# Second branch: queries projected before keys; x turned in pairs; nine early Z sums; fifth chunks prepared ahead

## The chip, the core and the metric

The kernel runs on one core of a Trainium2 chip. The core has a matrix engine (TensorE: PE for matmuls and transposes, PEld for its weight loads), VectorE (DVE), ScalarE (ACT), GpSimd (POOL) and SyncE (SP, which here only issues DMAs). Each engine takes its instructions in program order, and engines wait for each other through semaphores. The metric is device time in microseconds (us) of one execution; smaller is better.

## The reference

Two attention branches over the same tokens (S = 2048, D = 640, 32 heads of 20) are mixed by a gate. Cut to what matters here:

```python
x = A_x
g = sigmoid((x * gate_w).sum(-1, keepdims=True))
return g * A(x) + (1 - g) * B(x)

# A: linear attention with learned features
q, k, v = split_heads(x @ wqkv)
pq, pk = q @ w_phi, k @ w_phi                       # per head, 20 x 20
phi_q = concat(softmax(pq), softmax(-pq))
phi_k = concat(softmax(pk), softmax(-pk))
kv, z = phi_k.T @ v, phi_k.sum(tokens)
A = ((phi_q @ kv) / (phi_q @ z + 1e-6)) @ wo

# B: four segments of 512 tokens, a causal softmax and a memory (M, z)
phi = lambda t: where(t > 0, t + 1, exp(t))
for s in range(4):
    a_dot = causal_softmax(qs @ ks.T * 20 ** -0.5) @ vs
    a_mem = (phi(qs) @ M) / (phi(qs) @ z + 1e-6)
    outs.append(sigmoid(beta) * a_mem + (1 - sigmoid(beta)) * a_dot)
    M, z = M + phi(ks).T @ vs, z + phi(ks).sum(tokens)
B = concat(outs) @ wo_B
```

The inputs and the output are bf16.

## The kernel before

Tokens go in 16 chunks of 128, the 640 features in five blocks of 128 (KC), the 32 heads in eight groups of four. Both stages around the change run under an order written out by hand: instructions stand on each engine's queue as the code emits them. Lines are those of the kernel before.

**Start.** Weights of the first branch's keys come by DMA in five row blocks. For each block n, step T (`emit_foldT`, L175) transposes it on PE and evicts it; step M (`emit_foldM`, L182) multiplies it by `Wphi`, a block-diagonal copy of `w_phi` that POOL writes in five products (`emit_Wphi`, L142), and ACT evicts the product into `WkA`. Step X (`emit_xT`, L192) transposes one chunk of x (five PE transposes) and DVE copies it into `xTf`. The loop at L299 gives their order. All of these, the warm-up transposes (L296) and later `pk`, `pv`, `kv_ps`, `pq` use one PSUM pool of four double-bank buffers (tag `w2`), taken in turn.

**First branch, keys and values.** `emit_a1` (L226) runs 16 times: key and value projections of a chunk on PE (ten matmuls each, L232), two exponentials on ACT, sums and reciprocals on DVE, normalisation on POOL into `EkSn`, from where a DMA spreads it over the 32 tiles of `Z`. Then `kv` is formed on PE (L373) in tiles that DVE masks into `kvn` (L380), a tile's PSUM buffer coming free with that product. On DVE the 31 sums of the Z tiles (`emit_zadd`, L256, one instruction each) stand in three runs around the `kvn`: tiles 1 to 11, 12 and 13, 14 to 31. PE turns the sum later (`emit_z`), and DVE makes the denominators' operand `kvd` from it.

**First branch, queries.** `emit_pq` (L386) projects queries, ACT takes both exponentials (L398). A loop over the 16 chunks (from L570) forms numerators (`num`, L440), scales them on DVE (`tt`, L486), adds them on POOL (`oA`, L592) and turns the result by DMA into `oTA`. Between them `emit_next_half` puts projections of the second branch for its first chunks (L539, a half being 320 of 640 columns), evicted by ACT: the list `halves` holds chunks 0 to 3 of k and q and 0 to 7 of v, and ends with k and q of chunk 4. A finished k or q chunk is turned by DMA (`emit_turn`, L551) into `kTs` or `qTs`.

**Second branch.** 32 steps (4 segments, 8 groups of heads) go in 16 pairs; the loop is at L896. A pair has five bursts: each puts scores for four heads into two PSUM tiles (L666) and ACT takes two exponentials of 128x1024 into `PT` (L670); POOL zeroes the triangle above the diagonal (L677). Between the bursts the pair's other work is dealt out in the order of a string of `PLAN` (L882), by its estimated time:

- h: a projection half for the next segment (L854), evicted by DVE (L860); after a chunk's second half of q or k, its turn by DMA is issued, and its feature step is queued up. The order of the halves of segments 2 and 3 is `CHUNKED` (L870), that of segment 1 `FIRST_SEG`.
- x, y: DVE finishes phi of the oldest waiting k (x) or q (y) chunk: a minimum with 1 (L829), then maximum and sum (L830). The exponential they need is issued on ACT by `run_first(waiting[..])` (L920): one waiting q chunk behind burst 0, one waiting k chunk behind burst 2; in pair 0 behind bursts 2 and 3.
- z: SP issues the turn of phi(q) of that chunk into `xTf` (L839), out of the single staging tile `phiq_st`.
- A, B, C, D: the matmuls with V (L722, `pv_items`), for C and D also those with the memory (`mem_items`, L730 and L735) and the end of a step (`emit_epi`, L741): `rec`, `td`, `mtmp` on DVE, `oB`, `Msb`, `Mbd` on POOL. A and D belong to the pair's first step, B and C to the second step of the pair before. Their PSUM tile `nda` is single, so the next step's first matmul waits for `mtmp`, its last reader.
- o, f: output projections (L800); t, u: turns of finished outputs by DMA.

Of the kernel before, what the change touches and what calls it, by code (L numbers as in the profile page):

```python
# [7 lines left out]
ACT = mybir.ActivationFunctionType  # L8
# [7 lines left out]
def kernel(  # L16
# [15 lines left out]
    nc = tc.nc  # L32
# [109 lines left out]
    def emit_Wphi(j):  # L142
        h0, h1 = TH[j]
        nc.gpsimd.tensor_tensor(out=Wphi[:, j, 0:h1 - h0, :],
                                in0=Wc[:, j:j + 1, :].to_broadcast([P, h1 - h0, DH]),
                                in1=wmask[:, j, h0:h1, None].to_broadcast([P, h1 - h0, DH]),
                                op=ALU.mult)

    for j in range(KC):
        emit_Wphi(j)  # L150
# [41 lines left out]
    def emit_xT(sc, eng):  # L192
        tp = aps.tile([P, KC, P], BF16, name="xtp", tag="w2")
        for c in range(KC):
            nc.tensor.transpose(out=tp[:, c, :], in_=x_nat[sc // 2][:, sc % 2, c * P:(c + 1) * P],
                                identity=ident_b)
        eng(out=xq[:, sc // 4, :, sc % 4 * P:(sc % 4 + 1) * P], in_=tp)  # L197
# [28 lines left out]
    def emit_a1(sc):  # L226
        pk, pv = w2tile("pk"), w2tile("pv")
        for ps, W, n in ((pk, WkA, 320), (pv, WvA, 321)):
            for bk in range(2):
                for c in range(KC):  # L230
                    rhs = WvA[:, c, bk, :] if W is WvA else WkA[:, c, bk * 320:(bk + 1) * 320]
                    nc.tensor.matmul(ps[:, bk, 0:n], lhsT=key_tokens(c, sc), rhs=rhs,  # L232
                                     start=(c == 0), stop=(c == KC - 1))
# [62 lines left out]
    warm = aps.tile([P, KC, P], BF16, name="warm", tag="w2")  # L296
    for n in range(25):
        nc.tensor.transpose(out=warm[:, n % KC, :], in_=ident_b, identity=ident_b)
    for step in ("T0", "T1", "T2", "M0", "M1", "T3", "T4", "M2", "X0", "M3", "X1", "M4", "X2", "X3"):  # L299
        n = int(step[1])  # L300
        if step[0] == "T":
            emit_foldT(wnat_k, WkT, n, nc.scalar.copy if n == 1 else nc.vector.tensor_copy)
        elif step[0] == "M":
            emit_foldM(WkT, WkA, n)
        else:
            emit_xT(n, nc.vector.tensor_copy)
# [94 lines left out]
    emit_zadd(range(1, 12))  # L401
# [9 lines left out]
    emit_zadd(range(12, 14))  # L411
# [131 lines left out]
    def emit_half(pool, part, sc, half, eng, **kw):  # L543
        ps = pool.tile([P, 320], F32, name="proj", **kw)
        emit_half_mm(ps, part, sc, half)
        psv = ps.rearrange("p (h d) -> p h d", d=DH)
        hs = slice(half * 16, (half + 1) * 16)
        dst = vBs[(sc // 4) % 2][:, sc % 4] if part == "v" else stages[part][sc % 2]
        eng(out=dst[:, hs, 0:DH], in_=psv)

# [7 lines left out]
    for vB in vBs:  # L558
        nc.gpsimd.memset(vB[:, :, :, DH:DH + 1], 1.0)
    halves = [(part, c, half) for n in range(4) for part, c in (("k", n), ("q", n), ("v", n), ("v", 4 + n))  # L560
              for half in range(2)] + [(part, 4, half) for part in "kq" for half in range(2)]

    def emit_next_half():
        if halves:
            emit_half(last_pps if len(halves) % 3 == 1 else pps, *halves.pop(0), nc.scalar.copy)

    nums = [emit_num(0, 0)]
    emit_next_half()
    nums.append(emit_num(0, 1))
    for ch in range(NCH):  # L570
# [3 lines left out]
        part, c = (("k", ch // 4), ("q", ch // 4), ("v", ch // 4), ("v", 4 + ch // 4))[k]  # L574
# [26 lines left out]
        if k < 2:  # L601
            emit_turn(part, c, kT0 if part == "k" else qT0)
# [15 lines left out]
    with ExitStack() as bctx:  # L618
# [3 lines left out]
        Eqf = Eq0.rearrange("p j s t -> p (j s t)")  # L622
        kTs, qTs = ([t, Eqf[:, n * G * L:(n + 1) * G * L].rearrange("p (g t) -> p g t", g=G)]
                    for n, t in enumerate((kT0, qT0)))
# [12 lines left out]
        phiq_st = Eqf[:, 2 * G * L:2 * G * L + 2 * L].rearrange("p (h e) -> p h e", e=32)  # L637
# [182 lines left out]
        def features(part, sc):  # L820
# [3 lines left out]
            def exps():  # L824
                ek = bw.tile([P, H, DH], BF16, name="ek")
                nc.scalar.activation(out=ek, in_=src, func=ACT.Exp)  # L826
# [40 lines left out]
        def half_items(s, order):  # L867
            return [half_item(part, 4 * s + c, half) for part, c in order for half in range(2)]

        CHUNKED = [(part, c) for c in range(4) for part in "kqv"]  # L870
# [11 lines left out]
        PLAN = {0: ("hhhhoyzoAoxD", "hhBhyhzCooxAoD", "hhBhyhzCooxAoD", "ooBoyozCooxAoD"),  # L882
                1: ("hhBhhChxAhDtt", "hhBhyhzCfhhxAD", "hhBhyhzCfhhxADt", "hhBhyhzCfhhxAD"),
                2: ("hhBhyhzChxAhDt",) + ("hhBhyhzCfhhxADt",) * 3,
                3: ("fByfzCffADtt", "fBftCfftAD", "fBftCfffAD", "ufBfCfffAD")}
# [6 lines left out]
        for part in "kq":  # L892
            emit_turn(part, 4, (kTs if part == "k" else qTs)[1])
            features(part, 4)
        prev = None
        for dstep in range(NSEG * G // 2):  # L896
# [21 lines left out]
            for n, burst in enumerate(bursts(a, b)):  # L918
                burst()
                if n in ((0, 2) if dstep else (2, 3)):  # L920
                    run_first(waiting["kq"[n == (0 if dstep else 2)]])
                while items and (n == 4 or done + items[0][0] / 2 < (n + 1) * share):
                    w, fn = items.pop(0)
                    fn()
                    done += w
# [141 lines left out]
```

## Time and profile before

| what | us |
|---|---|
| median of 3 runs (lowest, highest) | 327.36 (327.29, 328.22) |
| the profiled execution, its own time | 326.66 |
| its span in the trace | 324.9 |
| exponentials of the scores (ACT, L670), 160 of them | 154.0 |
| matmuls with V (PE, L722) | 41.7 |
| exponentials of the waiting chunks (ACT, L826) | 0.74 each, 20 in the second branch's pairs |
| start to first key projection (PE, L232) | 10.7 |
| first exponential of the second branch's scores | 133.5 |
| start of pair 8 / of pair 9 | 223.2 / 235.5 |

The profile is of one execution: its span runs from the first to the last instruction in the trace, and its own time is 1.8 us longer. The costliest groups after the exponentials, with columns line, engine, operation, output<-input, count, then busy us and mean ns of one, then idle time ahead of it and what ended most of that:

```profile
L666 PE MATMUL st_ps<-Z 32*128 32x512 bf16 (+3 forms) x256 | 24.7, 299 | 3.7 <-ACT PT L670 3.1
L486 DVE TENSOR_TENSOR tt<-num,rr 128x640 f32<-128x640 f32 x32 | 24.8, 802 | 4.9 <-POOL rr L479 2.2
L800 PE MATMUL proj<-WkA,oTA 128*128 128x320 bf16 x160 | 27.1, 300 | 0.0
```

The last column tells who kept an engine waiting: the scores on PE wait for ACT to free their PSUM tiles, the scaled numerators wait for a POOL product, and the output projections wait for nothing.

### The profile page before, as it was taken

What the parts mean: (1) busy time and instruction counts of PE and PEld (TensorE: products, weight loads), DVE (VectorE), ACT (ScalarE), POOL (GpSimd) and SP (SyncE); (2) the same over time, 40 slices, a digit from 0 to 9 for tenths busy, and PEclk for the clock granted to TensorE, in tenths of its full rate; (3) what the DMA queues carried; (4) which work ended last, traced back from release to release, by engine and by line L of the source; (5) the groups of instructions that cost most, each with busy time, mean ns of one, the idle gap of its engine ahead of it and who ended that gap; (6) DMA issues with size and microseconds to landing.
All of it is one profiled execution on the core that took longest, in us unless ns stands there. A gap on an engine that the chain in (4) does not pass through costs nothing.

```text
span 324.9 us, 9495 instructions
## 1 busy us (share of the span) xinstructions
PE 308.9 (95%) x3904; PEld 212.9 (66%) x3904; DVE 223.0 (69%) x447; ACT 252.1 (78%) x322; POOL 211.2 (65%) x310
## 2 busy tenths in 40 slices
PE   7999999999999999989999999999799999999995
PEld 6788877964577788555565566655566656555663
DVE  2577997997799797377768567776575665454463
ACT  4677888138845555899999999999799889898853
POOL 8688599202268789647657667677776787666550
PEclk9999999999999999999999999999999999999999
DMA  7948935691015867766231455633555553422122
GB/s 226 201 112 195 209 98 154 194 366 39 0 34 105 117 106 124 147 121 84 52 67 32 87 55 67 139 56 65 87 79 92 103 104 39 113 67 58 46 87 81
DMA packets 91812, 34.19 MB, mean 105 GB/s; under 512 B 79866, under 2 KB 91770, under 8 KB 91770
## 3 DMA queue, kind: packets, MB, share of 16 engines
q1 hardware_dynamic: 91194, 32.95, 49.5%
q10 hardware_dynamic: 576, 0.66, 0.7%
q8 instruction: 30, 0.49, 0.6%
q14 instruction: 12, 0.10, 0.1%
HBM read 6.42 MB, written 2.62 MB: 28 GB/s over the span
## 4 chain that ended last, share of the span: by engine, by line
PE 41%; ACT 20%; issue 2%; DVE 1%; DMA 1%; SPq 0%; ACTq 0%; DVEq 0%
ACT PT L670 19%; PE st_ps L666 9%; PE proj L800 8%; PE proj L854 7%; PE nda L722 6%; PE proj L539 4%; PE num L440 2%; DMA xTf<-Eq 1%; PE nda L730 1%; PE nda L735 1%; ACT ek L826 1%; PE nda L976 1%; PE st_ps L976 0%; PE den L450 0%; DVE rec L747 0%
## 5 line engine op out<-in xcount | busy, mean ns | idle before, releaser
L670 ACT ACTIVATE PT<-st_ps 128x1024 bf16<-128x1024 f32 x160 | 154.0, 1025 | 15.1 <-PE st_ps L666 12.4
L677 POOL TENSOR_SCALAR_AFFINE_SELECT PT<-PT 128x512 bf16<-128x512 bf16 (+1 forms) x130 | 86.8, 685 | 48.7 <-ACT PT L670 48.4
L722 PEld LDWEIGHTS <-PT 128*128 128x128 bf16 x1280 | 40.1, 96 | 11.1 <-issue 6.4
L722 PE MATMUL nda<-vB,PT 128*128 128x21 bf16 x1240 | 41.7, 173 | 1.4 <-DVE mtmp L765 0.9
L244 POOL TENSOR_TENSOR EkSn<-Ek,krec 128x1280 bf16<-128x1280 bf16 x16 | 37.5, 2361 | 8.3 <-DVE krec L243 8.1
L854 PEld LDWEIGHTS <-xTf 128*128 128x128 bf16 x300 | 26.3, 97 | 16.0 <-issue 7.2
L860 DVE CAST Z<-proj 128x320 bf16<-128x320 f32 x44 | 20.7, 486 | 19.7 <-PE proj L854 19.4
L232 PEld LDWEIGHTS <-xTf 128*128 128x128 bf16 x240 | 27.1, 113 | 6.2 <-DVE xTf L197 0.7
L240 DVE TENSOR_REDUCE ksum<-Ek 128x64 f32<-128x1280 bf16 x16 | 23.6, 1475 | 8.0 <-ACT Ek L236 8.0
L236 ACT ACTIVATE Ek<-pk 128x640 bf16<-128x640 f32 x32 | 20.8, 702 | 10.6 <-PE pk L232 9.8
L666 PE MATMUL st_ps<-Z 32*128 32x512 bf16 (+3 forms) x256 | 24.7, 299 | 3.7 <-ACT PT L670 3.1
L486 DVE TENSOR_TENSOR tt<-num,rr 128x640 f32<-128x640 f32 x32 | 24.8, 802 | 4.9 <-POOL rr L479 2.2
L592 POOL TENSOR_TENSOR oA<-tt 128x640 bf16<-128x640 f32 x16 | 24.6, 1545 | 4.7 <-DVE tt L486 3.4
L800 PE MATMUL proj<-WkA,oTA 128*128 128x320 bf16 x160 | 27.1, 300 | 0.0
L666 PE MATMUL st_ps<-Eq 32*128 32x512 bf16 (+3 forms) x256 | 24.6, 299 | 2.2 <-ACT PT L670 1.7
L398 ACT ACTIVATE Eq<-pq 128x1024 bf16<-128x1024 f32 x20 | 19.4, 1021 | 5.4 <-PE pq L393 5.4
L762 POOL TENSOR_TENSOR oB<-td 128x320 bf16<-128x320 f32 x22 | 18.9, 861 | 5.9 <-DVE td L759 4.9
L800 PE MATMUL proj<-WvA,oT 128*128 128x320 bf16 x120 | 22.3, 300 | 0.5 <-DVE oTA L809 0.5
L393 PE MATMUL pq<-xTf,WqA 128*128 128x512 bf16 x100 | 22.1, 379 | 0.0
L759 DVE TENSOR_TENSOR td<-nda,rec 128x640 f32<-128x640 f32 x23 | 19.0, 825 | 2.1
L539 PEld LDWEIGHTS <-xTf 128*128 128x128 bf16 x180 | 16.3, 97 | 4.4
L232 PE MATMUL pk<-WkA,xTf 128*128 128x320 bf16 x120 | 18.3, 299 | 0.6 <-DVE xTf L197 0.6
(166 smaller groups left out, 551.7 us busy)
## 6 DMA issues: line engine op xcount, KB each, us to landing
Z<-EkSn SPq DMA_DIRECT2D x32, 160.0 KB, 2.7
out_dram<-orow SPq DMA_DIRECT2D x8, 160.0 KB, 2.0
out_dram<-oTA SPq DMA_DIRECT2D x6, 160.0 KB, 1.9
WvA<-in_A_wqkv_dram SPq DMA_DIRECT2D x2, 400.0 KB, 6.8
WkB<-in_B_wk_dram SPq DMA_DIRECT2D x1, 800.0 KB
WqB<-in_B_wq_dram SPq DMA_DIRECT2D x1, 800.0 KB, 7.0
WvB<-in_B_wv_dram SPq DMA_DIRECT2D x1, 800.0 KB, 8.6
WkA<-in_A_wo_dram SPq DMA_DIRECT2D x1, 800.0 KB, 11.3
```

What stands on the lines that cost most here:

```text
L232: nc.tensor.matmul(ps[:, bk, 0:n], lhsT=key_tokens(c, sc), rhs=rhs, start=(c == 0), stop=(c == KC - 1))
L240: nc.vector.tensor_reduce(out=ksum, in_=Ek.rearrange("p s (h f) -> p (s h) f", f=DH), axis=AX.X, op=ALU.add)
L244: nc.gpsimd.tensor_tensor(out=EkSn[:, sc].rearrange("p s (h f) -> p (s h) f", f=DH), in0=Ek.rearrange("p s (h f) -> p (s h) f", f=DH), in1 ...
L486: nc.vector.tensor_tensor(out=tt[:, sgn].rearrange("p (b h) d -> p b h d", b=2), in0=ps, in1=csb, op=ALU.mult)
L539: nc.tensor.matmul(ps, lhsT=xq[:, sc // 4, cc, sc % 4 * P:(sc % 4 + 1) * P], rhs=W[:, cc, half * 320:(half + 1) * 320], start=(cc == 0), s ...
L592: nc.gpsimd.tensor_tensor(out=oA.rearrange("p (h d) -> p h d", d=DH), in0=tt[:, 0], in1=tt[:, 1], op=ALU.add)
L666: nc.tensor.matmul(ps[:, i - i0, o:o + L - c * P], lhsT=kT[32 * i:32 * i + 32, c * P:(c + 1) * P], rhs=qT[32 * i:32 * i + 32, c * P:L], st ...
L670: nc.scalar.activation(out=PT[:, i0:i0 + 2], in_=ps, func=ACT.Exp, scale=SCALE_B)
L677: nc.gpsimd.affine_select(out=v, in_=v, pattern=[[0, n_i], [1, P]], compare_op=ALU.is_ge, fill=0.0, base=0, channel_multiplier=-1)
L722: nc.tensor.matmul(nd[:, j, i], lhsT=block(st, c)[:, i, (j - c) * P:(j - c + 1) * P], rhs=vB[:, c, 4 * st.g + i, :], start=(c == 0), stop= ...
L800: nc.tensor.matmul(ps, lhsT=oT[:, k % KC], rhs=W[:, k % KC, hs], start=(k == 0), stop=(k == n - 1))
L854: nc.tensor.matmul(ps, lhsT=xq[:, sc // 4, k, sc % 4 * P:(sc % 4 + 1) * P], rhs=W[:, k, half * 320:(half + 1) * 320], start=(k == 0), stop ...
```

## The change

Six things change; no instruction is dropped from the computation, and PE's matmuls and transposes keep their number.

1. `emit_Wphi` takes an engine. Blocks 0 and 2 go to DVE, 4, 1 and 3 to POOL, in the order 0, 4, 2, 1, 3.
2. `emit_xT` takes a pair of chunks: ten transposes into one double-bank PSUM tile, one copy by DVE instead of two. X0 and X1 now stand ahead of M3 and M4 in the steps, T4 is evicted by ACT, and the first `emit_a1` goes through its matmuls by input block with the two column halves inside.
3. The warm-up uses two PSUM tiles instead of one and x two instead of four, so every later user of the four `w2` buffers is shifted by one.
4. The first run of Z sums covers tiles 1 to 9 instead of 1 to 11, and the second tiles 10 to 13.
5. k and q of chunk 4 move in `halves` ahead of v of chunks 3 and 7; their turns are issued in the loop of the first branch; their exponentials are taken on ACT in the loop's last two rounds, into the places where phi is formed, and x and y of pair 0 find them done. Pair 0's two places for an exponential (now behind bursts 0 and 2) serve the next chunks. The last half is evicted by DVE.
6. `CHUNKED` becomes q, k, v for each chunk. In `PLAN` y and z move to the end of the pairs of segments 1 and 2 and x, where there is one, to their middle; in pair 0 an o moves behind y and z, and in pair 12 y and z go. From segment 1 on, burst 0 issues the exponential of k and burst 2 that of q; segment 0 keeps q first.

Counted on ACT, the exponentials of waiting chunks fall by pair as follows (pairs 0 to 12): before 2, 2, 2, 2, 1, 2, 2, 2, 1, 1, 1, 1, 1; after 1, 2, 2, 1, 1, 2, 2, 2, 2, 1, 1, 1, 0.

```diff
--- before.py
+++ after.py
@@ -139,15 +139,15 @@
     kvd = Aw.tile([P, 2, KC, H, 2], BF16, name="kvd")
     for j, (h0, h1) in enumerate(TH):
         nc.gpsimd.tensor_copy(out=wmw[:, j, 0:h1 - h0], in_=wmask[:, j, h0:h1])
-    def emit_Wphi(j):
+    def emit_Wphi(j, eng):
         h0, h1 = TH[j]
-        nc.gpsimd.tensor_tensor(out=Wphi[:, j, 0:h1 - h0, :],
+        eng.tensor_tensor(out=Wphi[:, j, 0:h1 - h0, :],
                                 in0=Wc[:, j:j + 1, :].to_broadcast([P, h1 - h0, DH]),
                                 in1=wmask[:, j, h0:h1, None].to_broadcast([P, h1 - h0, DH]),
                                 op=ALU.mult)
 
-    for j in range(KC):
-        emit_Wphi(j)
+    for j, eng in ((0, nc.vector), (4, nc.gpsimd), (2, nc.vector), (1, nc.gpsimd), (3, nc.gpsimd)):
+        emit_Wphi(j, eng)
...
@@ -189,12 +189,15 @@
                              start=(n in FIRST), stop=(n in LAST))
         nc.scalar.copy(out=dst[:, ic, :].rearrange("p (b n) -> p b n", b=2), in_=ps[:, :, 0:320])
 
-    def emit_xT(sc, eng):
-        tp = aps.tile([P, KC, P], BF16, name="xtp", tag="w2")
-        for c in range(KC):
-            nc.tensor.transpose(out=tp[:, c, :], in_=x_nat[sc // 2][:, sc % 2, c * P:(c + 1) * P],
-                                identity=ident_b)
-        eng(out=xq[:, sc // 4, :, sc % 4 * P:(sc % 4 + 1) * P], in_=tp)
+    def emit_xT(n):
+        pair = w2tile("xtp")
+        for u in range(2):
+            tp = pair[:, u].bitcast(BF16)[:, 0:D].rearrange("p (c t) -> p c t", c=KC)
+            for c in range(KC):
+                nc.tensor.transpose(out=tp[:, c, :], in_=x_nat[n][:, u, c * P:(c + 1) * P], identity=ident_b)
+        dst = xq[:, 0, :, 2 * n * P:2 * (n + 1) * P].rearrange("p c (u t) -> p u c t", u=2)
+        src = pair.bitcast(BF16)[:, :, 0:D].rearrange("p u (c t) -> p u c t", c=KC)
+        nc.vector.tensor_copy(out=dst, in_=src)
...
@@ -226,11 +229,11 @@
     def emit_a1(sc):
         pk, pv = w2tile("pk"), w2tile("pv")
         for ps, W, n in ((pk, WkA, 320), (pv, WvA, 321)):
-            for bk in range(2):
-                for c in range(KC):
-                    rhs = WvA[:, c, bk, :] if W is WvA else WkA[:, c, bk * 320:(bk + 1) * 320]
-                    nc.tensor.matmul(ps[:, bk, 0:n], lhsT=key_tokens(c, sc), rhs=rhs,
-                                     start=(c == 0), stop=(c == KC - 1))
+            by_row = [(c, bk) for c in range(KC) for bk in range(2)]
+            for c, bk in by_row if sc == 0 else sorted(by_row, key=lambda t: t[1]):
+                rhs = WvA[:, c, bk, :] if W is WvA else WkA[:, c, bk * 320:(bk + 1) * 320]
+                nc.tensor.matmul(ps[:, bk, 0:n], lhsT=key_tokens(c, sc), rhs=rhs,
+                                 start=(c == 0), stop=(c == KC - 1))
...
@@ -293,17 +296,17 @@
             op=ALU.mult)
         return omgh_b, CM
 
-    warm = aps.tile([P, KC, P], BF16, name="warm", tag="w2")
+    warm = [aps.tile([P, KC, P], BF16, name="warm", tag="w2") for _ in range(2)]
     for n in range(25):
-        nc.tensor.transpose(out=warm[:, n % KC, :], in_=ident_b, identity=ident_b)
-    for step in ("T0", "T1", "T2", "M0", "M1", "T3", "T4", "M2", "X0", "M3", "X1", "M4", "X2", "X3"):
+        nc.tensor.transpose(out=warm[n % 2][:, n % KC, :], in_=ident_b, identity=ident_b)
+    for step in ("T0", "T1", "T2", "M0", "M1", "T3", "T4", "M2", "X0", "X1", "M3", "M4"):
         n = int(step[1])
         if step[0] == "T":
-            emit_foldT(wnat_k, WkT, n, nc.scalar.copy if n == 1 else nc.vector.tensor_copy)
+            emit_foldT(wnat_k, WkT, n, nc.scalar.copy if n in (1, 4) else nc.vector.tensor_copy)
         elif step[0] == "M":
             emit_foldM(WkT, WkA, n)
         else:
-            emit_xT(n, nc.vector.tensor_copy)
+            emit_xT(n)
...
@@ -398,7 +401,7 @@
             nc.scalar.activation(out=Eq[:, sgn, :], in_=pqf, func=ACT.Exp, scale=1.0 - 2.0 * sgn)
         Eqs[qb, j] = Eq
 
-    emit_zadd(range(1, 12))
+    emit_zadd(range(1, 10))
     PAIRS = [(js, sgn) for js in ((0, 3), (1, 4)) for sgn in range(2)]
     for js, sgn in PAIRS:
         for j in js:
@@ -408,7 +411,7 @@
             emit_kv(j, sgn, range(14, NCH))
...
-    emit_zadd(range(12, 14))
+    emit_zadd(range(10, 14))
...
@@ -541,12 +544,15 @@
                              start=(cc == 0), stop=(cc == KC - 1))
 
     def emit_half(pool, part, sc, half, eng, **kw):
+
         ps = pool.tile([P, 320], F32, name="proj", **kw)
         emit_half_mm(ps, part, sc, half)
         psv = ps.rearrange("p (h d) -> p h d", d=DH)
         hs = slice(half * 16, (half + 1) * 16)
         dst = vBs[(sc // 4) % 2][:, sc % 4] if part == "v" else stages[part][sc % 2]
         eng(out=dst[:, hs, 0:DH], in_=psv)
+        if half == 1 and part in "kq":
+            turns_due.append((part, sc))
 
...
@@ -557,13 +563,20 @@
     nc.gpsimd.tensor_copy(out=Msb[:, :, :, DH], in_=epsm[:, None, :].to_broadcast([P, G, 4]))
     for vB in vBs:
         nc.gpsimd.memset(vB[:, :, :, DH:DH + 1], 1.0)
-    halves = [(part, c, half) for n in range(4) for part, c in (("k", n), ("q", n), ("v", n), ("v", 4 + n))
-              for half in range(2)] + [(part, 4, half) for part in "kq" for half in range(2)]
+    turns_due = []
+    halves = [(part, c, half) for n in range(4) for part, c in
+              (("k", n), ("q", n)) + ((("k", 4), ("q", 4)) if n == 3 else ()) + (("v", n), ("v", 4 + n))
+              for half in range(2)]
 
     def emit_next_half():
         if halves:
-            emit_half(last_pps if len(halves) % 3 == 1 else pps, *halves.pop(0), nc.scalar.copy)
-
+            emit_half(last_pps if len(halves) % 3 == 1 else pps, *halves.pop(0),
+                      nc.scalar.copy if halves else nc.vector.tensor_copy)
+
+    Eqf = Eq0.rearrange("p j s t -> p (j s t)")
+    kTs, qTs = ([t, Eqf[:, n * G * L:(n + 1) * G * L].rearrange("p (g t) -> p g t", g=G)]
+                for n, t in enumerate((kT0, qT0)))
+    phiq_st = Eqf[:, 2 * G * L:2 * G * L + 2 * L].rearrange("p (h e) -> p h e", e=32)
     nums = [emit_num(0, 0)]
     emit_next_half()
     nums.append(emit_num(0, 1))
@@ -571,7 +584,6 @@
         bt = next(n for n, chs in enumerate(BATCH) if ch in chs)
         k = ch - BATCH[bt][0]
         ahead = BATCH[bt + 1] if bt < len(BATCH) - 1 else None
-        part, c = (("k", ch // 4), ("q", ch // 4), ("v", ch // 4), ("v", 4 + ch // 4))[k]
         tt = a3w.tile([P, 2, H, DH], F32, name="tt")
         for sgn in range(2):
             emit_tt(tt, sgn, nums[sgn], cs_of[ch])
@@ -598,8 +610,13 @@
         if ahead and k == 2:
             nc.vector.reciprocal(out=dd, in_=dd)
             emit_cs(ahead, rr_n, dd)
-        if k < 2:
-            emit_turn(part, c, kT0 if part == "k" else qT0)
+        while turns_due:
+            part, c = turns_due.pop(0)
+            emit_turn(part, c, (kTs if part == "k" else qTs)[c // 4])
+        if ch >= NCH - 2:
+            part = "kq"[ch - NCH + 2]
+            nc.scalar.activation(out=(phiks[1][:, 0] if part == "k" else phiq_st)[:, :, 0:DH],
+                                 in_=stages[part][0][:, :, 0:DH], func=ACT.Exp)
         nc.sync.dma_start_transpose(out=oTA[:, ch], in_=oA)
         if k == 1:
             key = stages["k"][(ch // 4) % 2][:, :, 0:DH]
@@ -619,9 +636,6 @@
         bctx.enter_context(tc.manual_schedule(
             engines={mybir.EngineType.PE, mybir.EngineType.Activation, mybir.EngineType.DVE,
                      mybir.EngineType.Pool, mybir.EngineType.SP}))
-        Eqf = Eq0.rearrange("p j s t -> p (j s t)")
-        kTs, qTs = ([t, Eqf[:, n * G * L:(n + 1) * G * L].rearrange("p (g t) -> p g t", g=G)]
-                    for n, t in enumerate((kT0, qT0)))
...
@@ -822,8 +835,10 @@
             dst = phiks[(sc // 4) % 2][:, sc % 4] if part == "k" else phiq_st
 
             def exps():
-                ek = bw.tile([P, H, DH], BF16, name="ek")
-                nc.scalar.activation(out=ek, in_=src, func=ACT.Exp)
+                ek = dst[:, :, 0:DH]
+                if sc > 4:
+                    ek = bw.tile([P, H, DH], BF16, name="ek")
+                    nc.scalar.activation(out=ek, in_=src, func=ACT.Exp)
 
                 def rest():
                     nc.vector.tensor_scalar_min(out=ek, in0=ek, scalar1=1.0)
@@ -867,7 +882,7 @@
         def half_items(s, order):
             return [half_item(part, 4 * s + c, half) for part, c in order for half in range(2)]
 
-        CHUNKED = [(part, c) for c in range(4) for part in "kqv"]
+        CHUNKED = [(part, c) for c in range(4) for part in "qkv"]
         FIRST_SEG = [(part, c) for c in range(1, 4) for part in "kq"]
...
@@ -879,10 +894,10 @@
 
 
 
-        PLAN = {0: ("hhhhoyzoAoxD", "hhBhyhzCooxAoD", "hhBhyhzCooxAoD", "ooBoyozCooxAoD"),
-                1: ("hhBhhChxAhDtt", "hhBhyhzCfhhxAD", "hhBhyhzCfhhxADt", "hhBhyhzCfhhxAD"),
-                2: ("hhBhyhzChxAhDt",) + ("hhBhyhzCfhhxADt",) * 3,
-                3: ("fByfzCffADtt", "fBftCfftAD", "fBftCfffAD", "ufBfCfffAD")}
+        PLAN = {0: ("hhhhyzoxoAoD", "hhBhyhzCooxAoD", "hhBhyhzCooxAoD", "ooBoyozCooxAoD"),
+                1: ("hhBhhChhyzADtt", "hhBhxhCfhhyzAD", "hhBhxhCfhhyzADt", "hhBhxhCfhhyzAD"),
+                2: ("hhBhxhChhyzADt",) + ("hhBhhCfhhyzADt",) * 3,
+                3: ("fBfCffADtt", "fBftCfftAD", "fBftCfffAD", "ufBfCfffAD")}
 
         oT4 = oTA[:, 0:4]
 
@@ -890,8 +905,8 @@
             nc.sync.dma_start_transpose(out=oT4[:, n, 0:3], in_=oBs[NSEG - 1][:, n, 0:3 * P])
 
         for part in "kq":
-            emit_turn(part, 4, (kTs if part == "k" else qTs)[1])
             features(part, 4)
+            run_first(waiting[part])
         prev = None
         for dstep in range(NSEG * G // 2):
             s, gd = divmod(dstep, G // 2)
@@ -917,8 +932,8 @@
             done = 0.0
             for n, burst in enumerate(bursts(a, b)):
                 burst()
-                if n in ((0, 2) if dstep else (2, 3)):
-                    run_first(waiting["kq"[n == (0 if dstep else 2)]])
+                if n in (0, 2):
+                    run_first(waiting["kq"[n == (0 if s == 0 else 2)]])
                 while items and (n == 4 or done + items[0][0] / 2 < (n + 1) * share):
                     w, fn = items.pop(0)
                     fn()
```

1 line of the change is left out of this document (removed).

## The prediction

> **What bounds the kernel now.** First the busy times and the page's clock row: TensorE (PE) is busy 95% of the span at full granted clock, so time comes only out of PE's 16 us of idle or off the engines it alternates with.
>
> ```profile
> PE 308.9 (95%) x3904; PEld 212.9 (66%) x3904; DVE 223.0 (69%) x447; ACT 252.1 (78%) x322; POOL 211.2 (65%) x310
> ...
> PEclk9999999999999999999999999999999999999999
> ```
>
> Then the windows, cut at the first exponential of each pair of steps in the second branch (133.5 us on). I number these pairs 0 to 15, four to a segment. The columns are start:end, length, then the busy time of PE, PEld, DVE, ACT, POOL (x: instructions), the granted clock, DMA share and GB/s.
>
> ```profile
> 133.51:144.20 10.69, 9.57 (x109) 5.29 (x109) 5.49 (x11) 10.46 (x13) 5.61 (x8) 1.00 0.81 153
> 166.62:177.79 11.17, 10.62 (x158) 6.64 (x157) 8.30 (x20) 10.71 (x13) 7.24 (x13) 1.00 0.13 25
> 223.16:235.45 12.29, 10.11 (x162) 6.36 (x161) 7.27 (x17) 10.09 (x11) 9.52 (x18) 1.00 0.40 68
> 246.96:258.47 11.51, 11.39 (x171) 7.26 (x170) 7.47 (x17) 10.20 (x11) 8.23 (x15) 1.00 0.54 86
> ```
>
> Pairs 0 and 3 (rows one and two) lean on ACT, pair 10 (last) on PE. Pair 8, the first of segment 2, is the odd one: both engines have 10.1 us of work and it takes 12.29. The timeline there and the chain of waits say why.
>
> ```profile
> 229.35 1.24 SPq L553 DMA_TRANSPOSE Eq<-Z  x1
> ...
> 230.65 3.30 SPq L839 DMA_TRANSPOSE xTf<-Eq  x2
> ...
> 231.34 0.76 PE L722 MATMUL nda<-vB,PT 128*128 128x21 bf16 x24 [0.74 <-DVE mtmp L765]
> ...
> 234.66 0.21 PE L730 MATMUL nda<-Mbd,xTf 128*128 128x84 bf16 x1 [0.92 <-DMA xTf<-Eq]
> ...
> 235.45 1.02 ACT L670 ACTIVATE PT<-st_ps 128x1024 bf16<-128x1024 f32 x1 [0.97 <-PE st_ps L666]
> ```
>
> The turn of the last chunk of phi(q) is issued at 230.65, behind the key and query turns on SP; PE waits for it, and ACT for PE. Two more places where PE idles, from the timeline of the first branch:
>
> ```profile
> 9.78 0.89 DVE L197 COPY xTf<-xtp 128x640 bf16<-128x640 bf16 x2 [0.19 <-PE xtp L195]
> ...
> 10.73 1.55 PE L232 MATMUL pk<-WkA,xTf 128*128 128x320 bf16 x10 [0.60 <-DVE xTf L197]
> ...
> 56.97 7.94 DVE L258 TENSOR_TENSOR Z<-Z 128x640 bf16<-128x640 bf16 x11
> ...
> 64.82 1.77 DVE L380 TENSOR_TENSOR kvn<-kv_ps,wmw 128x140 bf16<-128x140 f32 x8
> ...
> 65.39 2.55 PE L373 MATMUL kv_ps<-vA,EkSn 128*128 128x80 bf16 x64 [0.80 <-DVE kvn L380]
> ```
>
> In both PE waits for DVE: for the last turned x, and for a PSUM buffer that kvn has yet to read, behind eleven sums.
>
> **The change part by part.**
>
> *Nine Z sums first.* The sums go at 0.527 us each (64.41 minus 59.67, by nine), so two fewer free DVE 1.05 us earlier, at 63.9. The first pair of kv tiles ends on PE at about 63.85; two kvn at a pitch of 0.21 (1.77 by 8) and 0.29 of length end at 64.4. PE would be free at 64.42 (last matmul 64.36, pitch 0.06), and starts at 64.46 instead of 65.39: **0.9**. The two sums come back after kvn; all sums still end near 77.6, and PE turns Z at 78.76 less 0.9, so 0.3 us of cover is left. Every later chain of the first branch (zt, kvd, den) starts from that turn and moves along. Bounds 0.6 (that cover fails) and 0.95.
>
> *x in pairs, Wphi on two engines, T4's eviction on ACT.* PE cannot pass 6.98 us, where T3 waits for the DMA that lands at 6.93; Wphi (five of 0.46 on POOL, done 6.05) is thus worth nothing earlier. From 6.98: ten transposes at 0.056 (7.54), M2 0.40 (7.94), first pair 0.56 (8.50); the second pair waits for x's second load, landed 8.72, and ends at 9.31. The paired copy does not occur before; two copies of 640 take 0.89 and share one fixed cost, so 0.82 to 0.89, and 1.6 if the 4-D pattern fell to the rate of the f32 evictions (320 in 0.49, as long as 640 bf16). I take 0.85, since layout and type are those of the 640 rows: 8.70 to 9.55, then to 10.40. The first projection starts at 10.45 instead of 10.73, and its value half is held to about 11.9 by WvA (landed 11.54, then 0.2 of copy): **0.2**. The by-row order lets M3 and M4 be evicted on ACT until 11.2 without a wait. Bounds -1.2 (1.6 per copy) and 0.3.
>
> *PSUM rotation.* By the built order the first num of the second stage takes the buffer that pq 3 held, not pq 2's; its exponentials end at 89.8, num starts at 91.0: 0, covered by 1.2 us; uncovered it would cost what is missing.
>
> *Early turns and exponentials of the fifth chunks.* Their halves move ahead of v, same matmul count; the turns enter SP earlier, past oTA turns whose takers come 15 us later. ACT gains two exponentials (0.72 long, pitch 0.63, from L610) and loses one eviction (0.42) to DVE, which ends its last tt at 132.4 and is free. Queued behind them is the first PT. Laying the evictions at 0.37 to 0.42 behind their matmuls from the relu triple's end (130.73), the last exponential ends at 133.4; PT needs its scores at 133.5 anyhow: 0, bounds 0 and -0.3. In pair 0 the second exponential (141.77) goes, but PE reaches the scores of pair 1 only at 143.62 without having idled after 142.28, so PT starts at 144.05 instead of 144.20: **0.15**, bounds 0.1 and 0.62. Pair 3 also loses its second one (the keys run one pair ahead), yet the scores behind it are ready only 0.06 before it ends: **0.06**, bounds 0 and 0.62.
>
> *Queries first.* phi(q) of a chunk is now formed in its own pair; its turn of pair 7 goes at 223.1 (min and sum end at 11.45 of the pair, as x's do now) and lands by 229, 4 us ahead of its reader. SP's next entry, the query turn of pair 8, is due at 225.4 and passes. Without a projection between A and D, two of them stand between C and A, so 0.68 of the 0.74 behind mtmp is filled. Pair 8 gets a second exponential: ACT 10.09+0.62, with the 0.41 of idle that pairs 1 to 3 keep: 11.15, as pair 2 takes 11.17 with the same ACT work and more PE. From 12.29: **1.1**, bounds 0.35 and 1.3.
>
> *phi(q) at the end of pairs 9 to 11.* min and sum (0.32+0.82) now stand there ahead of rec. In pairs 6 and 7 another part's do: rec starts at 11.35 instead of 11.13, and the pairs take 11.55 instead of 11.51: 3 x 0.04, **-0.1**. Pairs 5 to 7 and 12 to 15 keep their work.
>
> Sum: 0.9 + 0.2 + 0.15 + 0.06 + 1.1 - 0.1 = 2.3 us. The profiled execution took 326.66 (span 324.9 and 1.8 around it), the median of the runs is 327.36, 0.7 above. 326.66 - 2.3 = 324.4; against the median **325.1**, which I forecast.
>
> **The rivals.**
>
> *The exponentials pay in full.* If PE's chain in pairs 0 and 3 yields with ACT's, 0.62 twice replaces 0.21: 3.3 us, **324.0**. For it: ACT is busy 10.46 of 10.69 in pair 0. Against: the scores behind both come at the same moment as now.
>
> *A new wait in pair 8.* If its other gaps stay (2.20 of ACT idle less the 0.97 of the transfer), it takes 10.09 + 0.62 + 1.23 = 11.94 and gains 0.35: **325.8**. For it: mtmp, with nda single-buffered. Against: the projections that now fill it.
>
> *The paired copies run at half rate:* -1.2 in place of 0.2, 0.9 in all: **326.5**, within 0.3%, which is about what this kernel's runs can tell from no change. Against: 640 bf16 in the time of 320 f32.
>
> *Slower: the late sum collides with POOL.* phi(q)'s sum took 1.20 to 1.29 instead of 0.82 in pairs 1 to 3 and 8, each beside a POOL mask that took 3.05 for four. At the end of pairs 4 to 11 it would push rec, td and mtmp by 0.45, and the next pair's PE waits for mtmp already (0.16 in pair 9), so from the first delay on it counts in full: 8 x 0.45 = 3.6, **328.7**. Against: the sums that stand there now took 0.82 in every pair. The Trainium skill (SBUF — State Buffer, "SBUF: two separate sides") says that a VectorE operation with two SBUF inputs and a GpSimd one that reads SBUF exclude each other for a whole instruction. The trace agrees at 56.97, where the first Z sum took 2.67 us beside a 2.36 us POOL product; by that rule any overlap at the pair's end gives this rival's time.
>
> **How the numbers follow.** Forecast 0.56, exponentials in full 0.17, new wait 0.12, half-rate copies 0.08, slower 0.07. The likeliest one's own range is 324.3 to 325.9; with the second and third case, 323.8 to 326.6, which leaves out about 0.15. Faster by over 0.3% (under 326.4): 0.56 + 0.17 + 0.10 = 0.83; within: 0.02 + 0.08 = 0.10; slower 0.07.
>
> **What would show it.** PE's wait on kvn under 0.15; the first projection near 10.5, and paired copies of 0.85; the first PT near 132.4; pair 8 at 11.2 with no wait for xTf; pairs 9 to 11 at 11.55. Wrong, if rec in those pairs starts after 11.5, if the paired copy takes over 1.2, or if the second branch as a whole is no shorter than its 189 us.

## The result and the profile after

The changed kernel takes 324.03 us (median of 4 runs, 323.78 to 324.17), the kernel before 327.57 (4 runs, 327.29 to 328.22): a ratio of 0.9888, 95% interval 0.9871 to 0.9906. That is 3.5 us less, where 2.3 was forecast from 327.36. The two profiled executions, however, differ by only 2.5 us: 326.66 and 324.17. So one us of the gain is not in this pair of profiles, and the experiments begin there.

First the engines' row of the changed kernel's page, and the same four windows as before, cut at the first exponential of pairs 0, 3, 8 and 10 (start:end, length, busy time of PE, PEld, DVE, ACT, POOL, granted clock, DMA share, GB/s):

```profile
PE 309.2 (96%) x3901; PEld 213.5 (66%) x3904; DVE 224.7 (70%) x447; ACT 252.1 (78%) x322; POOL 208.5 (65%) x308
```

```profile
132.25:142.85 10.60, 9.40 (x112) 5.21 (x111) 6.19 (x14) 9.99 (x13) 6.39 (x9) 1.00 0.92 138
165.18:176.35 11.17, 10.62 (x158) 6.63 (x157) 8.31 (x20) 10.10 (x11) 7.24 (x13) 1.00 0.13 25
221.80:232.77 10.97, 10.17 (x161) 6.38 (x160) 8.55 (x19) 10.51 (x13) 8.82 (x15) 1.00 0.39 73
244.19:255.90 11.71, 11.55 (x171) 7.21 (x170) 7.48 (x18) 10.31 (x12) 7.92 (x15) 1.00 0.60 83
```

PE's work is what it was, in a span 2.5 us shorter. Pair 8 lost 1.32 us, with ACT 0.42 busier. Pairs 0 and 3 are nearly as long as before although ACT has 0.5 and 0.6 us less to do in them: the exponential taken out there left idle time on ACT. Pair 10 grew by 0.2. The timeline shows the two places of the first branch and the transition into the second:

```profile
8.93 1.56 DVE L200 COPY xTf<-xtp 128x1280 bf16<-128x1280 bf16 x2 [0.89 <-PE xtp L197]
...
10.54 1.55 PE L235 MATMUL pk<-WkA,xTf 128*128 128x320 bf16 x10 [0.19 <-DVE xTf L200]
...
56.45 10.44 PE L376 MATMUL kv_ps<-vA,EkSn 128*128 128x140 bf16 x192
...
63.77 1.78 DVE L383 TENSOR_TENSOR kvn<-kv_ps,wmw 128x140 bf16<-128x140 f32 x8
...
125.61 1.26 SPq L559 DMA_TRANSPOSE Z<-Z  x1
...
131.82 0.40 PE L679 MATMUL st_ps<-Z 32*128 32x512 bf16 x4
...
132.25 1.94 ACT L683 ACTIVATE PT<-st_ps 128x1024 bf16<-128x1024 f32 x2
```

The two paired copies take 1.56 us together (0.82 each by the trace, overlapping a little); the kv matmuls run through as one group of 192 where PE waited 0.80 us before; `kvn` starts 1.05 earlier. The line at 125.61 is the turn of q chunk 3, the last of the first segment (the expectations below call it the third q chunk). It now leaves SP six us ahead of the first scores (131.82). And pair 8:

```profile
221.71 2.74 SPq L854 DMA_TRANSPOSE xTf<-Eq  x2
...
229.60 0.23 DVE L778 TENSOR_TENSOR mtmp<-nda,CM 128x84 f32<-128x84 f32 x1
...
230.85 1.18 PE L735 MATMUL nda<-vB,PT 128*128 128x21 bf16 x40
...
231.88 0.31 PE L743 MATMUL nda<-Mbd,xTf 128*128 128x84 bf16 x4
...
232.77 1.94 ACT L683 ACTIVATE PT<-st_ps 128x1024 bf16<-128x1024 f32 x2 [0.46 <-POOL oB L775]
```

The turns of phi(q) are issued ten us ahead of their reader at 231.88, which waits for nothing, and `mtmp` ends a full us ahead of the next step's matmuls.

### The profile page after: what moved, and what is told of

Read it like the earlier page. It is cut to its first block, busy times and chain, and to the rows that moved or that the text cites. A ratio compares the mean times of both kernels' runs of the same rounds, so it can differ in the third digit from the quotient of the medians.

```text
span 322.4 us, 9493 instructions
## 1 busy us (share of the span) xinstructions
PE 309.2 (96%) x3901; PEld 213.5 (66%) x3904; DVE 224.7 (70%) x447; ACT 252.1 (78%) x322; POOL 208.5 (65%) x308
## 4 chain that ended last, share of the span: by engine, by line
PE 37%; ACT 22%; DVE 3%; issue 2%; POOL 0%; ACTq 0%; DVEq 0%
ACT PT L683 19%; PE st_ps L679 9%; PE proj L813 7%; PE nda L735 6%; PE proj L869 5%; PE proj L542 3%; PE num L443 2%; DVE td L772 1%; PE nda L748 1%; PE nda L743 1%; DVE rec L762 1%; ACT ek L841 1%; PE nda L991 1%; DVE rec L760 1%; DVE Eq L845 1%
## 5 line engine op out<-in xcount | busy, mean ns | idle before, releaser
L690 POOL TENSOR_SCALAR_AFFINE_SELECT PT<-PT 128x512 bf16<-128x512 bf16 (+1 forms) x130 | 85.4, 675 | 48.5 <-ACT PT L683 48.3
L443 PE MATMUL num<-kvn,Eq 128*128 128x240 bf16 (+2 forms) x192 | 18.0, 229 | 0.6 <-DVE tt L489 0.6
```

Of the source, the lines that this page charges most:

```text
L443: nc.tensor.matmul(t[:, bk, (lo - 16 * bk) * DH:(hi - 16 * bk) * DH], lhsT=Eqs[qb, j][:, sgn, qc * P:(qc + 1) * P], rhs=kvn[:, sgn, j, lo ...
L690: nc.gpsimd.affine_select(out=v, in_=v, pattern=[[0, n_i], [1, P]], compare_op=ALU.is_ge, fill=0.0, base=0, channel_multiplier=-1)
```

## The experiments

Each ran beside the kernel before on the same chip. Times are medians; the ratio is to the kernel before, with its 95% interval.

| run | us | ratio | profiled execution |
|---|---|---|---|
| kernel before, again | 327.20 | 1.000 (0.9992 to 1.0009) | 327.58 |
| changed, again | 323.81 | 0.9894 (0.9879 to 0.9909) | 323.74 |
| changed, eleven sums | 325.09 | 0.9933 (0.9921 to 0.9946) | 325.19 |
| changed, keys first | 325.24 | 0.9934 (0.9919 to 0.9948) | 325.24 |
| changed, start as before | 324.55 | 0.9913 (0.9900 to 0.9927) | 324.07 |
| changed, late exponentials | 324.44 | 0.9920 (0.9898 to 0.9943) | 324.78 |
| changed, turns late | 325.26 | 0.9936 (0.9921 to 0.9950) | 325.37 |
| before, early turns only | 326.41 | 0.9987 (0.9968 to 1.0006) | 326.17 |
| changed, y and z in the middle | 344.56 | 1.0531 (1.0513 to 1.0549) | 344.58 |
| changed, only y in the middle | 323.52 | 0.9886 (0.9870 to 0.9901) | 323.48 |
| changed, pair 0's first o late | 325.59 | 0.9950 (0.9936 to 0.9964) | 325.91 |
| changed, both of the last two | 325.83 | 0.9950 (0.9933 to 0.9967) | 325.91 |

**Both kernels a second time.** No edit.

> The kernel before, unchanged. The two profiles differ by 2.5 us (326.66 to 324.17), the medians by 3.5. Theory 'one fast execution': the first profile of before caught one of its faster executions, some wait on a transfer varies in it. Then a new profile has a span of 325.5 to 326.4 instead of 324.9, and a cut by pairs shows where the added us lies. Rival 'offset': executions of before that are not profiled are always 0.6 to 1.5 us slower than profiled ones; then the span is 324.9 again, and every pair as long as it was.

> The changed kernel, unchanged, on the chip of the three below. Its first profile has no wait for a turn ahead of the scores or in pair 8; if its gain is that these waits are gone, its executions spread little and its profile repeats: 42.3 us from the first num to the first exponential, pair 8 at 10.97, 324.0, ratio 0.989. Rival: the 3.5 us were partly one chip's, ratio 0.992 (2.5 us).

The first profile of before caught one of its shorter executions (326.66; the eleven beside the second profile took 326.95 to 327.88). Cut into stretches, the two profiles of each kernel read (us):

| stretch | before 1 | before 2 | changed 1 | changed 2 |
|---|---|---|---|---|
| start to first key projection | 10.73 | 10.66 | 10.54 | 10.29 |
| to first num | 80.27 | 80.31 | 79.41 | 79.40 |
| to first exponential of scores | 42.51 | 43.20 | 42.30 | 42.29 |
| pairs 0 to 7 | 89.65 | 89.64 | 89.55 | 89.56 |
| pair 8 | 12.29 | 12.54 | 10.97 | 10.97 |
| pairs 9 to 12 | 45.90 | 45.89 | 46.04 | 45.88 |
| pair 13 to the end | 43.59 | 43.59 | 43.61 | 43.60 |

Before varies in two stretches, both times at a transfer: pair 8, and the way to the first exponential. This is the timeline of the second profile of before:

```profile
126.58 2.44 SPq L553 DMA_TRANSPOSE Z<-Z  x1
...
130.44 1.26 SPq L553 DMA_TRANSPOSE Z<-Z  x1
...
133.74 0.40 PE L666 MATMUL st_ps<-Z 32*128 32x512 bf16 x4 [0.85 <-issue]
...
134.17 1.02 ACT L670 ACTIVATE PT<-st_ps 128x1024 bf16<-128x1024 f32 x1 [0.81 <-PE st_ps L666]
```

And these lines, from the first profile, are what the prediction should have read:

```profile
126.62 1.70 SPq L553 DMA_TRANSPOSE Z<-Z  x1
...
129.75 1.26 SPq L553 DMA_TRANSPOSE Z<-Z  x1
...
133.08 0.40 PE L666 MATMUL st_ps<-Z 32*128 32x512 bf16 x4 [0.16 <-issue]
```

The second SP line of each is the turn of q chunk 3. By the trace it landed at 132.99 in the first profile and at 133.65 in the second; the first scores started 0.09 later both times. They read q from that transfer. The profile puts the wait down to "issue", so nothing in the row names the DMA; only the landing time does. Between the profiles an issue on SP took 2.44 instead of 1.70, everything behind it on SP slid, and the whole second branch with it.

The trace also shows what stands beside that long issue. The page of before counts, among its DMA queues:

```profile
q8 instruction: 30, 0.49, 0.6%
```

These are 30 transfers of 16 KB each, of the kind that the page calls instruction. One of them ends at 127.21 in the first profile and at 127.90 in the second, and the long issue ends 1.11 us later each time. Pair 8 varies the same way. PE's wait there ends 0.04 us after the first of two turns of phi(q) has landed, at 234.62 in the first profile and 235.52 in the second. That is 3.97 and 4.21 us after its issue began, and 1.1 after the end of another of the 16 KB transfers; in the two profiles of the changed kernel the same turn lands after 2.55 and 2.32. Counted from the start of the pair, that transfer ends 0.24 later in the second profile of before, which is what the pair grew by.

**The turn by itself.** Two runs: the changed kernel with its turns at their places of before, and the kernel before with early turns only.

```diff
 # changed, turns late
-        while turns_due:
-            part, c = turns_due.pop(0)
-            emit_turn(part, c, (kTs if part == "k" else qTs)[c // 4])
+        if k < 2:
+            emit_turn("kq"[k], ch // 4, (kTs, qTs)[k][0])
+        if ch >= NCH - 2:
+            emit_turn("kq"[ch - NCH + 2], 4, (kTs, qTs)[ch - NCH + 2][1])
 # before, early turns only (turns_due filled in emit_half for chunks 0 to 3)
-        if k < 2:
-            emit_turn(part, c, kT0 if part == "k" else qT0)
+        while turns_due:
+            part, c = turns_due.pop(0)
+            emit_turn(part, c, kT0 if part == "k" else qT0)
```

> The changed kernel with the turns of chunks 0 to 3 issued at their places of before (first and second round of each four), and those of chunk 4 in the last two rounds. Theory 'the turn': the first scores wait for the third q chunk's turn again, 42.4 to 43.3 us lie between the first num and the first exponential, differing from one execution to the next: 324.2 to 325.0. Rival 'the exponentials': 42.3 as in the changed kernel, 324.0.

> The kernel before with one part of the change: turns of chunks 0 to 3 issued in the round in which the second half is projected. Theory 'the turn': 42.4 from the first num to the first exponential instead of 42.51 (first profile) and 43.20 (second), 0.1 to 0.8 faster, by the medians about 0.5: 326.7. Rival 'the exponentials': 327.26, nothing gained.

Both came out by the turn: 43.00 us from the first num to the first exponential with late turns, 42.29 in the kernel before with early ones, as in every other profile with early turns. Timeline of the changed kernel with late turns:

```profile
129.06 1.27 SPq L559 DMA_TRANSPOSE Z<-Z  x1
...
132.38 0.40 PE L680 MATMUL st_ps<-Z 32*128 32x512 bf16 x4 [0.65 <-DVE vB L553]
...
138.56 0.99 PE L814 MATMUL proj<-WkA,oTA 128*128 128x320 bf16 x6 [1.01 <-DMA oTA<-oA]
```

The turn landed at 132.29, again 0.09 ahead of the scores (this time the row blames DVE). The last line is a second price: the turn of the last `oA`, further back on SP, is now waited for by pair 0's first output projection, and the pair takes 11.24 instead of 10.60. The kernel before with early turns gained 0.8 us by the medians; its interval still touches 1, because its executions spread from 326.09 to 329.75.

**Late exponentials.**

```diff
-              (("k", n), ("q", n)) + ((("k", 4), ("q", 4)) if n == 3 else ()) + (("v", n), ("v", 4 + n))
-              for half in range(2)]
+              (("k", n), ("q", n), ("v", n), ("v", 4 + n))
+              for half in range(2)] + [(part, 4, half) for part in "kq" for half in range(2)]
...
-                      nc.scalar.copy if halves else nc.vector.tensor_copy)
+                      nc.scalar.copy)
...
-        if ch >= NCH - 2:
-            part = "kq"[ch - NCH + 2]
-            nc.scalar.activation(...)
```

(With it, the exponentials, their places and the string of pair 0 are those of before.)

> The changed kernel with k and q of chunk 4 last in the list of halves again, all evicted by ACT, and their exponentials behind bursts 2 and 3 of pair 0; turns are still issued in the round in which a chunk's second half is projected. Two profiles of before had the first scores at 133.08 and 133.74, each 0.09 after the turn of the third q chunk landed (132.99, 133.65). Theory 'the turn': that transfer, not ACT, holds the first scores; with the turn early they stay early, the second branch starts 42.3 to 42.4 behind the first num as in the changed kernel (42.30), only pairs 0 and 1 get their 0.1 each back, 324.2. Rival 'the exponentials': ACT's work at the transition decides, the stretch is 42.5 or more again and 0.62 in pair 0 counts: 324.9.

42.29 us to the first exponential, with ACT's work at the transition as before: the exponentials have no part in that stretch. Pairs 0 and 1 take more than forecast, 10.84 and 11.51 instead of 10.60 and 11.17. In pair 0, 0.16 of the 0.24 is a longer wait of PE for the turn of an `oA` (0.50 instead of 0.34), which leaves about 0.08 for the exponential. Why pair 1 is longer than even the 11.25 of before was not followed up.

**Eleven sums, keys first, the start.** The edits put back `emit_zadd(range(1, 12))` and `range(12, 14)`; `CHUNKED` as "kqv" with the strings of segments 1 to 3 and q behind burst 0; and items 1 to 3 of the change.

> The changed kernel with eleven sums in the first run again. If nine sums are worth what the profile shows there (kvn 1.05 us earlier, 0.12 of it from the start): PE waits 0.8 us for kvn again and the time is 324.03 + 0.9 = 324.9. Rival: DVE's work is only moved, and the Z sums behind kvn (which end 0.4 us ahead of the turn on PE) take the gain back: 324.1. Rival 'the missing 1 us is here': 326.

> The changed kernel with keys first again in segments 2 and 3, and with the strings and the places of the exponentials of segments 1 to 3 as before. If the order of the projections is what shortens pair 8: pair 8 takes 12.3 instead of 10.97, pairs 9 to 11 together 34.53 instead of 34.69, and the time is 324.03 + 1.15 = 325.2. Rival: pair 8 is short because its work comes in earlier by the other parts, pair 8 stays near 11: 324.1. Rival 'the missing 1 us is here', a wait for the turn of phi(q) that varies from one execution to the next: 326.2, and executions that spread over 1 us.

> The changed kernel with the start as before: Wphi on POOL, x in four single turns, T4's eviction on DVE, the first key projections by column half, one warm-up tile. If the start is worth what the profile shows: first key projection at 10.73 instead of 10.54, and 0.1 to 0.2 us more, 324.2. Rival 'the missing 1 us is here': 325.2, and executions that spread over 1 us.

With eleven sums, the timeline has the wait again:

```profile
64.99 1.77 DVE L383 TENSOR_TENSOR kvn<-kv_ps,wmw 128x140 bf16<-128x140 f32 x8
...
65.55 2.55 PE L376 MATMUL kv_ps<-vA,EkSn 128*128 128x80 bf16 x64 [0.84 <-DVE kvn L383]
```

From the first key projection to the first num it takes 80.45 us, 1.04 more than the changed kernel. With keys first, the window of pair 8 and the reader of the last phi(q) turn in it:

```profile
221.67:234.03 12.36, 10.11 (x162) 6.36 (x161) 7.28 (x17) 10.09 (x11) 9.59 (x18) 1.00 0.41 66
```

```profile
233.25 0.21 PE L743 MATMUL nda<-Mbd,xTf 128*128 128x84 bf16 x1 [0.99 <-DMA xTf<-Eq]
```

The row of before returns almost digit for digit, with its wait for the transfer, although the start, the sums and the turns are those of the change. So it is the sixth part of the change that makes pair 8 short: the order of the projections with the strings of `PLAN` and the places of the exponentials. This run undoes the three together and does not tell them apart. The start is the unclear one: in its profile the start loses nothing (first key projection 10.55), and pair 0 takes 10.76 instead of 10.60, PE waiting 0.54 us instead of 0.34 ahead of the first output projection. Its other three executions are 0.4 to 0.6 us slower than that one. The first key projection of all profiles lies at 10.45 to 10.73 with the old start (four profiles, mean 10.60) and at 10.18 to 10.72 with the new one (ten, mean 10.41), with landings of the last weight block that differ by 0.7 (6.45 to 7.19). A gain of 0.19 fits that, but the two groups overlap; the 0.5 to 0.7 by which its median lies above the two of the changed kernel is not explained.

**Further moves of y, z and o.**

```diff
-  1: ("hhBhhChhyzADtt", "hhBhxhCfhhyzAD", "hhBhxhCfhhyzADt", "hhBhxhCfhhyzAD"),
-  2: ("hhBhxhChhyzADt",) + ("hhBhhCfhhyzADt",) * 3,
+  1: ("hhBhhChhyzADtt", "hhBhxhCfyhhzAD", "hhBhxhCfyhhzADt", "hhBhxhCfyhhzAD"),
+  2: ("hhBhxhChhyzADt",) + ("hhBhhCfyhhzADt",) * 3,
```

This is the version with y alone; in the one with both, yz stands in place of y. The third replaces pair 0's string "hhhhyzoxoAoD" by "hhhhyzxAoooD", the fourth joins the first and the third.

> The changed kernel with y and z of pairs 5 to 7 and 9 to 11 moved from the pair's end to the place behind the first f, ahead of the projections. If phi(q) at the end of these pairs costs the 0.17 of idle that PE gained in pairs 9 to 11 (34.69 us together, 34.53 before): back to 34.5 and 0.2 to 0.4 less in all, 323.8. Rival 'collision': the sum now runs beside POOL's masks in mid-pair, takes 1.2 instead of 0.83 and delays the evictions of projections behind it on DVE, 324.4.

> The changed kernel with y alone (minimum and sum of phi(q)) of pairs 5 to 7 and 9 to 11 behind the first f, z left where it is, behind the projections whose x it overwrites. If y at the pair's end costs PE what pairs 9 to 11 lost (34.69 us together, 34.53 in the kernel before): 34.5, and pairs 6 and 7 at 11.51, 0.2 less, 323.8. Rival 'collision': beside POOL's masks the sum takes 1.2 instead of 0.83 and holds up the evictions behind it, no gain or up to 0.4 more.

> The changed kernel with pair 0's first o behind A. In its profile PE waits 0.34 us there for the turn of the last oA (landed 137.27). If that wait counts, pair 0 takes 10.3 instead of 10.60: 323.7. Rival: pair 0 goes by ACT (0.59 idle of 10.60), whose scores come no earlier, 324.0.

> Both of the above. If they are independent and both count: 0.5 less than the changed kernel, 323.5; if neither, 324.0.

With y and z in the middle, v of segment 2 is computed from overwritten x: the turn of phi(q) writes where x of the same chunk lies, and now comes ahead of the v projections. These wait for it, in pairs 5 to 7 (17.98, 18.70 and 18.95 us instead of 11.5), and the granted clock of these pairs is 0.81 to 0.82. As v comes out of the wrong x, its time says nothing of this order. The timeline shows the wait in pair 5:

```profile
199.63 2.31 PE L869 MATMUL proj<-WvB,xTf 128*128 128x320 bf16 x8 [5.16 <-DMA xTf<-Eq]
```

With y alone in the middle, pairs 6 and 7 take 11.52 instead of 11.56 and pairs 10 and 11 take 11.47 instead of 11.56; the profiles differ by 0.26 (323.74 and 323.48) and the medians by 0.29, with intervals that overlap. It is the fastest version that ran, but the runs don't separate it from the changed kernel. Its timeline in pair 9, the only one of these pairs in which this happens, shows the collision that the prediction feared, without a price:

```profile
240.37 1.01 POOL L775 TENSOR_TENSOR oB<-td 128x320 bf16<-128x320 f32 x1
...
240.69 1.36 DVE L845 SCALAR_TENSOR_TENSOR Eq<-Z,ek 128x640 bf16<-128x640 bf16 x1
241.33 0.94 POOL L781 TENSOR_TENSOR Msb<-Msb,mtmp 128x84 f32<-128x84 f32 x1
```

The sum takes 1.36 instead of 0.83 and POOL's product beside it 0.94 instead of 0.36; in mid-pair nobody waits for either. The late o went the other way. In the timeline of pair 0:

```profile
138.88 0.43 PE L735 MATMUL nda<-vB,PT 128*128 128x21 bf16 x10 [1.83 <-POOL PT L690]
```

A now stands where the output projection gave POOL time for its masks; pair 0 takes 12.77 instead of 10.60. Not all of this is the wait: right behind it the granted clock falls, to 0.50 between 139 and 141 us and 0.87 over the pair, and PE is busy for 10.38 us in it instead of 9.40. Executions of this run at a clock of 1.0 took 325.31 to 325.36, those at 0.993 to 0.995 took 325.81 to 326.16: of the loss against 323.81, about 1.5 us comes without the slower clock and about 0.5 with it. The wait of 0.34 for the transfer that this was to save had been cheap. The fourth run shows the same in pair 0 (12.61 us, clock 0.87) and adds nothing to it.

## Why the prediction was right, and where its sum was off

The measured 324.03 lies below the 324.3 to 325.9 that the likeliest case was given by itself, and within the 323.8 to 326.6 of the three likeliest together. The two largest terms, the sums and pair 8, came out by the mechanisms that were named for them; a third gain, at the transition, came from a wait that the prediction had not seen.

- *Nine sums:* forecast 0.9, measured 0.86 and 0.91 by the first key projection to the first num, 1.04 when undone. No wait for `kvn` was left, and the 0.3 us of cover for the turn of Z held (sums end 77.33, PE turns at 77.72).
- *Start:* forecast 0.2; the first key projection came 0.19 earlier in the first profiles and in the mean of all, which the scatter between executions (0.5 with the new start alone) does not let count as shown. The paired copy takes 0.82, so half rate is refuted. That PE "cannot pass 6.98" was one execution's landing: in others that weight lands as early as 6.45.
- *Early turns and exponentials:* the step that failed. It gave the transition "0, bounds 0 and -0.3", since "PT needs its scores at 133.5 anyhow". The cover was itself a wait: the scores were held by the turn of q chunk 3, and the change moves that turn four us ahead (three against the first num). It is worth 0.2 against the first profile and 0.9 against the second. The moved transfers were judged by those they were moved past, and not by who waits for them.
- *The base:* the 0.7 us between the profiled execution and the median of before was carried to the new time as a constant. Between the two profiles of before, the difference is the same turn and pair 8's transfer being later. That most executions are like the second profile is inferred from their times; the others were not profiled. In the changed kernel both waits are gone, and its profiles lie on its runs (324.17 and 324.03, 323.74 and 323.81). The 1.1 us between 325.1 and 324.03 are these 0.7, the 0.2 by which the two profiles differ more than the sum of 2.3, and 0.14 by which the new median lies below its profile. In the 0.2 the turn and pair 8 stand for 0.22 each, and the other terms take about as much as one of them back.
- *Pairs 0 and 3:* forecast 0.15 and 0.06, measured 0.09 and 0.00; pair 1 gained 0.08. Pair 4, which got no term, takes 0.07 more. The rival "the exponentials pay in full" gave 324.0, the time that came out, by a mechanism that is refuted: its two pairs give 0.09 in place of 1.24.
- *Pair 8:* forecast 1.1 to a length of 11.2; it takes 10.97 in all profiles with queries first, 1.3 to 1.6 less. The prediction had the turn of phi(q) late because it stands behind the others on SP. That is one half. The other is the slow landing: after 2.4 us instead of 3.97 it would have been there at about 233.0, ahead of 233.74, where PE began to wait (an estimate from the landings in the changed kernel). The rival's new wait behind `mtmp` isn't there. The added exponential raised ACT's busy time by 0.42, not 0.62, and its idle is 0.46 (0.41 forecast).
- *Pairs 9 to 11:* forecast -0.1; -0.16 in the first profile and none in the second (34.69, 34.53, before 34.53). `rec` starts 11.22 to 11.50 us into these pairs, so the sign of being wrong at 11.5 was just not reached. The other sign speaks of 189 us for the second branch; from the first exponential to the end it took 191.4 us and now takes 190.2.
- *Collision with POOL:* at the ends of pairs 5 to 7 and 9 to 11 the sum takes 0.82 or 0.83, and POOL's next mask mostly starts 0.60 into it. In pairs 4 and 8 it takes 1.13, beside a mask; pair 4 is 0.07 longer, pair 8 is the short one. At these places the rival's 3.6 us do not arise. That the two slow each other down when they do meet is shown by the run with y in the middle: the sum lost 0.53 there, about what was left of the 0.86 that POOL's sum takes elsewhere, when it started 0.32 into it (beside it, POOL's sum took 1.01). This agrees with the Trainium skill (SBUF — State Buffer, "SBUF: two separate sides"), by which the second of two such operations waits for the whole first one; the price depends on who waits for the second, and there it was nobody.

## What to carry to other kernels

Where a stage starts "just when its operands are ready", look up when each operand's transfer landed: a wait that the profile puts down to issue or to an innocent engine can be a DMA queue's, and the queue's order is then worth more than the engines' work beside it. A difference between the profiled execution and the median is not a constant to be added: take a second profile and see which stretch differs, for the change may remove just that. And before moving a filler off a place because it waits there, ask what runs behind its cover.

## What the runs showed of the hardware

In all 14 profiles, the issue of a transposing DMA that starts on SP between 125.6 and 128.3 us took 1.7 to 2.4 us where most others take 1.2 to 1.3, whichever turn stood there (k, q or `oA`). It differed by 0.7 between two executions of the same kernel and shifted all that was queued behind it. In each of the 14 it ended 1.07 to 1.11 us after one of the 16 KB transfers of the instruction queue had ended.

It is not alone. Later than 95 us into the span, the 14 traces hold 99 issues of transposing DMAs of over 1.5 us, five to nine in each; every one overlaps such a 16 KB transfer, and of the 865 that overlap none, none took over 1.45. Another 128 overlap one and took under 1.5. That the issue waits for the transfer is read from this coincidence and from the fixed distance between their ends; no run moved such a transfer. Landings can be late with it, as the turn of phi(q) in pair 8 of before shows. What follows for a kernel: a turn that leaves SP well ahead of its reader is not exposed to it, as here the turns of q chunk 3 and of phi(q) no longer are.
